# A fused mLSTM, leaky MoE layer and top-1 MoE: the gates' pieces stored before the weight conversions, first loads reordered, and the front's schedule drawn anew

## The chip, the cores and the metric

One core of a Trainium2 chip. Times are device microseconds (us) of one execution. PE is TensorE (matmuls; PEld its weight loads), DVE VectorE, ACT ScalarE, POOL GpSimd, SP the engine that here only issues DMAs. ACT and POOL issue DMAs as well.

## The reference

```python
# mLSTM: B, H, S, D = 4, 8, 768, 40; one step per t
m_new = np.maximum(f_gate[:, :, t] + m, i_gate[:, :, t])
f_stab = np.exp(f_gate[:, :, t] + m - m_new); i_stab = np.exp(i_gate[:, :, t] - m_new)
C = f_stab * C + i_stab * einsum('bhd,bhe->bhde', vt, kt)
n = f_stab * n + i_stab * kt
y[:, :, t] = sigmoid(o_gate) * (C @ qt) / max(|n . qt|, 1)
# layer 1: x is (3072, 320), w_in (320, 2048), w_out (2048, 320)
h = x @ w_in; x = (max(h, 0) + alpha * min(h, 0)) @ w_out
# layer 2: expert = argmax of the cosine logits over 8 experts, gate = its softmax weight
out[mask] = gate * (max(x[mask] @ w1[e], 0) @ w2[e])      # w1[e] (320, 1024), w2[e] (1024, 320)
```

## The kernel before, in words

**Three stages.** The tokens are 24 chunks of 128 (6 for each of the 4 batches). Stage one, the mLSTM, works chunk by chunk. Stage two, the leaky layer, works on groups: chunk 0, chunk 1, then pairs of chunks. For group j and k = 0 to 7 the step `m1(j,k)` is 16 or 32 matmuls of the first product (L747); it is followed on ACT by `m1r` (L754), on DVE by two instructions `m1f` (L760, one for each half), on ACT by `m1h` (L764) and on POOL by `m1l` (L767). `m2(j,t,q)` is a quarter of the second product (12 matmuls, L835). Then come the router, a sort of the tokens by expert, and stage three, the experts (L1212, L1232). All products are of float16 pairs (a high and a low part), so nearly every tile is split in two.

**The gates** are done once, for all chunks, at the start. `g_load` brings f_gate and i_gate, `g_scan` (DVE, L295 to L299) makes running sums and maxima. From these come two things. First, each of two rows is cut into three bfloat16 pieces: `g_top` (ACT, L302), `g_res` (DVE, L305), `g_mid` (ACT, L309), `g_low` (DVE, L312), then `g_store` (SP, L315) writes them to `pc_d` in DRAM, and `g_rows` (L319) and `a_mrow` (L421) read them back in another layout as operands of `a_arg`, the first matmul that a chunk's decay matrix needs (L444, L446). Second, `g_w` (L324 to L326), `g_wexp` (ACT, L329), `g_wt` (PE, L336) and `g_wt2` (DVE, L340, L341) make the weights `wuT` and `winT` of the state; `g_dec` (L344) and `g_dec2` (L347) carry a column through DRAM to `decB`.

**A chunk i**: `load` (keys, values, gates: `kvo_t`, L411), `loadt` (queries and keys transposed: `qk`, L417), `arg` and `exp` (ACT, L453), scores `s` (PE, L462), `p` (DVE, L477: scores times decay), `phi` (ACT) and `plo` (POOL) split that, `vhi` and `vlo` (ACT L424, DVE L428) split the values, `vw` (POOL, L437) and `u` (PE, L472) make the state's update, `c` (DVE, L508) the state, `o` (PE, L516 to L523) the output, `tot` (DVE, L538 to L546), `th`, `y`, `yr`, and `xhi`, `xlo`, `xt` (ACT L560, DVE L564 and L566, an SP transpose L571) hand it to stage two. There are 48 `p` in all, two for each chunk.

**The weights of stage two** come as 64-bit floats in 26 pieces. `pload` (ACT's DMA queue, L690) brings a piece into one of 5 buffers, `pconv` turns two pieces into float32 with six DVE instructions (L637, L639, L641: 128x512 for the five pairs of w_in, 128x320 for the eight of w_out; I call one pair a conversion), `psplit` (ACT) and `plow` (POOL) split them, and two pieces with the tail rows of w_in are moved by `pput` (four SP DMAs, L668 to L671). The first steps of group 0 and 1 need their w_in pieces, their `m2` the w_out pieces. The weights of stage three are split in 56 units (`ul`, `uh`, `uo` on DVE at L1156 to L1160, `us`), scattered over stage two.

**What sets the order.** Every step is announced with `add(key, engine, cost, function, after=..., take=..., give=..., dma=..., at=...)`. `Plan.order` then plays a list schedule when the program is built: each step's rank is the longest path of costs behind it plus `lean(k)`, a number for each kind of step from the tables LEAN, SOON (chunks or groups 0 to 3, and steps without an index below 4) and FIRST (0 and 1), and it emits the steps in the order of its own clock. `at` is the earliest time there. On the chip each engine then runs its instructions strictly in that order; costs and ranks only decide the order. Each DMA also takes the next of eight semaphores in turn, so a DMA can't be issued before the one eight places ahead of it in the program has landed.

## Time and profile before

| | |
|---|---|
| median of 3 runs | 726.04 us (726.01 to 727.79) |
| profiled execution | 729.88 us, span 728.2 us |
| mean granted TensorE clock | 0.977 |
| PE busy | 639.3 us, 88% |
| PEld busy | 526.2 us, 72% |
| DVE busy | 470.0 us, 65% |
| ACT, POOL busy | 335.8 us (46%), 352.3 us (48%) |
| HBM | 143.57 MB read, 30.46 MB written, 239 GB/s over the span |

An engine's busy time is an average over stages: the sections below read it by stretches. Times of the trace count from the span's start.

### The profile page before, as it was taken

The page shows a single profiled execution, that of the slowest core. Times are in us where ns is not written, and L with a number is a line of the kernel's source. Part 1 is how long each engine was busy: PE and PEld are TensorE (multiplying, and loading weights), DVE is VectorE, ACT ScalarE, POOL GpSimd, SP SyncE. Part 2 cuts the span into 40 slices and gives each one's busy share as a digit, 9 for nine tenths or more (in the row PEclk, how much of TensorE's full clock was granted, in tenths as well). Part 3 has the DMA queues.
Part 4 walks back from the last instruction along what each step waited for, and adds up shares of the span by engine and source line. Part 5 has one row for each costly group of instructions (what it writes and reads, how often), then busy time and mean ns, then how long its engine had stood idle before and what let it go on. Part 6 is the DMA issues. An engine that isn't in the chain of part 4 may idle for free. (4 is left out here: it accounts for less than half of the span.)

```text
span 728.2 us, 17807 instructions
## 1 busy us (share of the span) xinstructions
PE 639.3 (88%) x6903; PEld 526.2 (72%) x6903; DVE 470.0 (65%) x1119; ACT 335.8 (46%) x666; POOL 352.3 (48%) x424
## 2 busy tenths in 40 slices
PE   1038468999999989999999999999989999989995
PEld 1025457778887867787878778887777888878884
DVE  8647997798888878888787888797145321112111
ACT  2434466666756576566665655344122222212221
POOL 6647575875646455656465646246112322323322
PEclk9997779999999999999999999999999999999999
DMA  8964343968869687868767675366793999999863
GB/s 233 210 181 136 123 136 82 230 194 197 226 179 292 164 232 184 250 202 247 204 216 220 197 207 163 84 272 153 199 269 86 258 287 282 296 283 340 206 198 69
DMA packets 107306, 149.03 MB, mean 205 GB/s; under 512 B 70295, under 2 KB 82496, under 8 KB 103378
## 3 DMA queue, kind: packets, MB, share of 16 engines
q1 hardware_dynamic: 79810, 83.22, 44.0%
q10 hardware_dynamic: 24128, 54.54, 23.8%
q0 software_dynamic: 3280, 10.10, 5.2%
q8 instruction: 56, 0.92, 0.5%
q14 instruction: 32, 0.26, 0.1%
HBM read 143.57 MB, written 30.46 MB: 239 GB/s over the span
## 5 line engine op out<-in xcount | busy, mean ns | idle before, releaser
L747 PE MATMUL hp<-xt,w_in_p 128*128 128x256 f16 (+1 forms) x1664 | 187.4, 268 | 16.3 <-DVE r L760 7.9
L747 PEld LDWEIGHTS <-w_in_p 128*128 128x128 f16 x1664 | 151.6, 100 | 39.5 <-DVE r L760 14.4
L767 POOL TENSOR_TENSOR g<-r,g 128x512 f16<-128x512 f32 (+1 forms) x104 | 122.6, 1185 | 112.4 <-ACT g L764 109.3
L835 PE MATMUL o<-w_out_p,g 128*128 128x320 f16 x1152 | 169.5, 299 | 0.0
L835 PEld LDWEIGHTS <-g 128*128 128x128 f16 x1152 | 111.8, 98 | 41.9
L1221 DVE SCALAR_TENSOR_TENSOR h<-hp,h 128x512 f16<-128x512 f32 x48 | 32.9, 690 | 114.3 <-ACT h L1217 114.3
L760 DVE SCALAR_TENSOR_TENSOR r<-r,al,hp 128x256 f32<-128x256 f32 (+1 forms) x208 | 84.6, 452 | 26.3 <-ACT r L754 26.0
L764 ACT ACTIVATE g<-r 128x512 f16<-128x512 f32 (+1 forms) x104 | 61.7, 595 | 76.4 <-DVE r L760 63.7
L485 POOL TENSOR_TENSOR ph<-mb,ph 128x512 f16<-128x512 f32 x48 | 63.2, 1323 | 41.3 <-ACT ph L482 40.6
L1232 PEld LDWEIGHTS <-h 128*128 128x128 f16 x648 | 61.8, 98 | 27.1 <-issue 4.4
L754 ACT ACTIVATE r<-hp 128x512 f32<-128x512 f32 (+1 forms) x104 | 57.5, 555 | 26.8 <-PE hp L747 20.7
L1217 ACT ACTIVATE h<-hp 128x512 f16<-128x512 f32 x48 | 28.3, 596 | 86.4 <-PE hp L1212 86.2
L1238 POOL DMA_INDIRECT out_dram<-y,idx x27 | 27.5, 1017 | 82.7 <-DMA out_dram<-y,idx 65.4
L1187 POOL DMA_INDIRECT xg<-x_d,idx x31 | 30.5, 985 | 57.6 <-ACT y L1235 51.9
L1212 PEld LDWEIGHTS <-wr 128*128 128x128 f16 x896 | 51.8, 98 | 2.6 <-issue 1.2
L1212 PEld LDWEIGHTS <-w_in_p 128*128 128x128 f16 x832 | 48.3, 98 | 1.4
L1212 PE MATMUL hp<-xt,wr 128*128 128x128 f16 x768 | 46.8, 219 | 1.0 <-ACT y L1235 0.6
L1212 PE MATMUL hp<-xt,w_in_p 128*128 128x128 f16 x768 | 46.8, 219 | 0.0
L1232 PE MATMUL o<-wr,h 128*128 128x320 f16 x288 | 42.9, 299 | 3.4 <-DMA wr<-wp 2.0
L1232 PE MATMUL o<-w_out_p,h 128*128 128x320 f16 x288 | 43.0, 299 | 1.1 <-DVE h L1221 0.6
L462 PE MATMUL sp<-qk 64*128 64x128 f32 x384 | 29.8, 293 | 15.3 <-DMA qk<-in_qk_t_dram 13.6
L472 PE MATMUL up<-vw,kvo_t 128*128 128x82 f32 x160 | 23.1, 292 | 22.1 <-POOL vw L438 16.0
(206 smaller groups left out, 1027.6 us busy)
## 6 DMA issues: line engine op xcount, KB each, us to landing
wr<-wp SPq DMA_DIRECT2D x32, 1280.0 KB
w_in_p<-wp SPq DMA_DIRECT2D x15, 1280.0 KB
w_out_p<-wp SPq DMA_DIRECT2D x15, 1280.0 KB
kvo_t<-in_kvo_dram SPq DMA_DIRECT2D x24, 576.0 KB
ust<-in_moe_w_dram ACTq DMA_DIRECT2D x32, 320.0 KB
wp<-wo ACTq DMA_DIRECT2D x32, 320.0 KB
ust<-in_moe_w_dram ACTq DMA_DIRECT2D x16, 512.0 KB
wp<-wo ACTq DMA_DIRECT2D x16, 512.0 KB
```

What stands on the lines that cost most here:

```text
L462: T.matmul(sp[:, r, z], lhsT=x[w, 1, z], rhs=x[w, 0, z], start=True, stop=True)
L485: G.tensor_tensor(st["P", i][:, 1, j], st["mb", i][:, j], st["P", i][:, 0, j], ALU.subtract)
L747: T.matmul(hp[:, a, :n], lhsT=w_in_p[:, wk, f], rhs=xt[:, xk], start=z == 0, stop=z == 7)
L754: A.activation(r, e_t[j, m], AF.Relu, scale=-1.0)
L760: V.scalar_tensor_tensor(r[:, a], r[:, a], al1[:, m + a:m + a + 1], hp[:, a], ALU.mult, ALU.add)
L764: A.activation(g_t[j][:, 0, m:m + 2], e_t[j, m], AF.Copy)
L767: G.tensor_tensor(g_t[j][:, 1, m:m + 2], e_t.pop((j, m)), g_t[j][:, 0, m:m + 2], ALU.subtract)
L835: T.matmul(o[:, :DM], lhsT=g[:, gi, k, tt], rhs=w_out_p[:, k, a], start=z == 0, stop=z == 47)
L1187: G.indirect_dma_start(out=xg, out_offset=None, in_=src, in_offset=bass.IndirectOffsetOnAxis(ap=idx[:, j:j + 1].bitcast(U32), axis=0))
L1212: T.matmul(hp[:, m], lhsT=w[:, wk, f], rhs=xt[:, xk], start=z == 0, stop=z == 7)
L1221: V.scalar_tensor_tensor(hs[:, 1], hp, 0.0, hs[:, 0], ALU.max, ALU.subtract)
L1232: T.matmul(o, lhsT=h[:, hi, k], rhs=w[:, k, a], start=z == 0, stop=z == 23)
```

## The change

Seven edits, all but the second and the third in what the plan is told:

- `g_low(1)` comes behind `g_low(0)`, and the first `pconv` behind `g_low(1)` in the list of dependences of piece 0's pair; the tables LEAN, SOON and FIRST have new numbers throughout, and some costs are raised.
- `g_w` runs on DVE and not on POOL.
- `xhi` and `x2_hi` write the 64 columns DM to DM+64 by a second ACT instruction, straight from their source; the DVE copies at L566 and L905 go.
- `load(i)` and `loadt(i)` wait for `load(i-1)` and `loadt(i-1)` in the plan, and those of chunks 1 and 2 are not placed before 14 and 26.
- `g_dec2` waits for `g_rows`.
- `alpha`, `rload` and `x2zero` are held to 20, 75 and 75, `consts` (the sort's constants) to 200.
- The units are told to start at 132.6 with 5.47 between them (115.5 and 5.75 before), with 2.07 (6.16) as the gap of their DVE steps.

```diff
-    START = {"T": 0.5, "V": 7.0, "A": 1.0, "G": 8.0, "S": 1.0}
+    START = {"T": 0.5, "V": 9.3, "A": 1.0, "G": 8.0, "S": 1.0}
...
 LEAN = {
-    "alpha": 150, "alpha2": 111.9, "arg0": -42.1, "arg1": -22.1, "c": 12.3, "cd": -127.5, "consts": -37.5,
+    "alpha": 82.5, "alpha2": 101, "arg0": -42.5, "arg1": -18.3, "c": -57.9, "cd": -81.1, "consts": -111.5,
...
-PACE = 6.16
-UNITS = (115.5, 5.75)
+PACE = 2.07
+UNITS = (132.6, 5.47)
...
-        G.tensor_tensor(mprev, last, gc[:, :NC_ - 1, P - 1:P], ALU.add)
-        G.tensor_tensor(ww[:, 1], aa[:, :NC_ - 1, :], last.to_broadcast([32, NC_ - 1, P]), ALU.subtract)
-        G.tensor_tensor(ww[:, 0], mprev.to_broadcast([32, NC_ - 1, P]), mm[:, 1:, :], ALU.subtract)
+        V.tensor_tensor(mprev, last, gc[:, :NC_ - 1, P - 1:P], ALU.add)
+        V.tensor_tensor(ww[:, 1], aa[:, :NC_ - 1, :], last.to_broadcast([32, NC_ - 1, P]), ALU.subtract)
+        V.tensor_tensor(ww[:, 0], mprev.to_broadcast([32, NC_ - 1, P]), mm[:, 1:, :], ALU.subtract)
...
-        A.activation(xs[i % NB][:, 0:DM], st["y", i], AF.Copy, scale=128.0)
+        x, y = xs[i % NB], st["y", i]
+        A.activation(x[:, 0:DM], y, AF.Copy, scale=128.0)
+        A.activation(x[:, DM:DM + 64], y[:, DM - 64:], AF.Copy, scale=128.0)
...
-        V.tensor_copy(x[:, DM:DM + 64], x[:, DM - 64:DM])
...
-          + ([("u", i - 3)] if (i - 3) % NC_ < NC_ - 1 else []), dma=1.8)
-        a("loadt", "S", 0.78, a_loadt, [(n, i - NQ) for n in ("s", "o")], dma=1.0)
+          + ([("u", i - 3)] if (i - 3) % NC_ < NC_ - 1 else []) + [("load", i - 1), ("loadt", i - 1)], dma=2.2, at=(0.0, 14.0, 26.0)[i] if i < 3 else 0.0)
+        a("loadt", "S", 0.78, a_loadt, [(n, i - NQ) for n in ("s", "o")] + [("load", i - 1), ("loadt", i - 1)], dma=1.2, at=(0.0, 14.0, 26.0)[i] if i < 3 else 0.0)
...
-                add(("pconv", z // 2), "V", 0.3 + 2.75 * c, p_conv, z, z + 1, after=[("pload", z), ("pload", z + 1)],
+                add(("pconv", z // 2), "V", 0.3 + 2.75 * c, p_conv, z, z + 1, after=[("pload", z), ("pload", z + 1)] + ([] if z else [("g_low", 1)]),
...
-        add(("g_low", a), "V", 0.85, g_low, a, after=[("g_mid", a)])
+        add(("g_low", a), "V", 0.95, g_low, a, after=[("g_mid", a)] + ([("g_low", 0)] if a else []))
...
-    add(("g_w",), "G", 5.3, g_w, after=[("g_scan",)])
+    add(("g_w",), "V", 2.2, g_w, after=[("g_scan",)])
...
-    add(("g_dec2",), "S", 3.0, g_dec2, after=[("g_dec",)], dma=0.3)
-    add(("alpha",), "S", 0.6, alpha_load, dma=0.1)
+    add(("g_dec2",), "S", 0.5, g_dec2, after=[("g_dec",), ("g_rows",)], dma=0.3)
+    add(("alpha",), "S", 0.4, alpha_load, dma=0.1, at=20.0)
...
-    add(("rload",), "S", 0.76, load_router, dma=0.1)
+    add(("rload",), "S", 0.76, load_router, dma=0.1, at=75.0)
...
-    add(("consts",), "G", 3.0, sort_consts, at=100.0)
+    add(("consts",), "G", 3.0, sort_consts, at=200.0)
```

What this does to the order shows on SP first: the program's start, just behind the program's entry, up to the third or fourth chunk load. Before (the two gates, then `qk` of chunks 0, 2 and 1, then `kvo_t`):

```order
L1288 DMA al_153<-in_moe_alpha_dram 128x16
L286 DMA gates_a<-in_f_gate_dram 32x768
L287 DMA gates_a<-in_i_gate_dram 32x768
L417 DMA qk_102<-in_qk_t_dram 40x1024 x2
L417 DMA qk_104<-in_qk_t_dram 40x1024 x2
L417 DMA qk_103<-in_qk_t_dram 40x1024 x2
L411 DMA kvo_t<-in_kvo_dram 128x1152 x2
L868 DMA em<-in_moe_expert_emb_dram 8x320
```

The changed program at the same place, and on to the gates' stores and their reading back:

```order
L286 DMA gates_a<-in_f_gate_dram 32x768
L287 DMA gates_a<-in_i_gate_dram 32x768
L411 DMA kvo_t<-in_kvo_dram 128x1152
L417 DMA qk_102<-in_qk_t_dram 40x1024 x2
L411 DMA kvo_t<-in_kvo_dram 128x1152
L417 DMA qk_103<-in_qk_t_dram 40x1024 x2
L344 DMA dec_d<-gates_b 32x4x1
L1289 DMA al_153<-in_moe_alpha_dram 128x16
L315 DMA pc_d<-gates_a 32x6x768
```

Chunk 0's `kvo_t` has moved from behind nine DMAs to the third place, and `alpha` and the router's loads have left the start. The next place on SP is the store of the pieces (`pc_d`) and its reading back. Before, it stands behind `decB` and the router's transpose, some DMAs later:

```order
L344 DMA dec_d<-gates_b 32x4x1
L892 DMA_TRANSPOSE enp<-ep 128x5x128
L347 DMA decB<-dec_d 128x128
L315 DMA pc_d<-gates_a 32x6x768
L319 DMA argL<-pc_d 8x4x768 x3
L421 DMA argR_113<-pc_d 3x8x128
```

In the changed program, from the store on:

```order
L315 DMA pc_d<-gates_a 32x6x768
L669 DMA w_in_p<-ttl 64x512
L670 DMA w_in_p<-ttl 64x512
L671 DMA w_in_p<-ttl 64x512
L672 DMA w_in_p<-ttl 64x512
L417 DMA qk_104<-in_qk_t_dram 40x1024 x2
L421 DMA argR_113<-pc_d 3x8x128
L319 DMA argL<-pc_d 8x4x768 x3
L421 DMA argR_114<-pc_d 3x8x128
L411 DMA kvo_t<-in_kvo_dram 128x1152
L347 DMA decB<-dec_d 128x128
```

The store now stands ahead of `decB`, which follows the reading back, and the four DMAs of one tail piece and chunk 2's `qk` stand between the store and the reading back. On DVE the place is the end of the gates' work. Before, the last instructions ahead of `wuT` are those of a fourth conversion:

```order
L639 SCALAR_TENSOR_TENSOR w_335<-wst,w_335 128x512
L639 SCALAR_TENSOR_TENSOR w_336<-wst,w_336 128x512
L641 SCALAR_TENSOR_TENSOR w_335<-wst,w_335 128x512
L641 SCALAR_TENSOR_TENSOR w_336<-wst,w_336 128x512
L340 TENSOR_SCALAR wuT<-gps 128x160
L341 COPY winT<-gps 128x160
L477 SCALAR_TENSOR_TENSOR mb<-sp,mb 128x512 x2
```

In the changed program one conversion (w_253 and w_254) stands ahead of `wuT`, between `g_res` and `g_low`:

```order
L642 SCALAR_TENSOR_TENSOR w_253<-wst,w_253 128x512
L642 SCALAR_TENSOR_TENSOR w_254<-wst,w_254 128x512
L312 TENSOR_TENSOR gates_a<-gates_a 32x768
L428 SCALAR_TENSOR_TENSOR vs_106<-kvo_t,vs_106 128x8x40
L312 TENSOR_TENSOR gates_a<-gates_b,gates_a 32x768
L1292 TENSOR_SCALAR al_153<-al_153 128x16
L340 TENSOR_SCALAR wuT<-gps 128x160
L341 COPY winT<-gps 128x160
L638 TENSOR_SCALAR w_287<-wst 128x512
```

Ahead of these rows DVE has, behind `g_scan`: `vlo(0)`, the three instructions of `g_w`, the two of `g_res` and the first conversion. Three more conversions follow before chunk 0's `tot` (L541), the third between chunk 0's two `p`; before the change five conversions of 128x512 and one of 128x320 and the router's eleven instructions (L880 to L888) stood ahead of that `tot`. ACT's first instructions are now `vhi(0)` and `th(0)`, then `g_top` twice, `g_wexp` and `g_mid` twice.

## Rows read from the trace of the kernel before

**Rows 1.** Stretches: length; busy (count) of PE, PEld, DVE, ACT, POOL; clock; DMA share, GB/s.
```profile
0.00:48.06 48.06, 6.10 (x34) 5.19 (x34) 32.50 (x61) 16.21 (x27) 31.26 (x50) 1.00 0.88 211
48.06:60.31 12.25, 8.53 (x48) 3.86 (x48) 9.44 (x14) 7.02 (x15) 5.47 (x5) 0.86 0.42 128
60.31:123.91 63.60, 44.16 (x494) 37.62 (x494) 54.53 (x121) 33.06 (x81) 43.06 (x103) 0.79 0.46 130
...
200.00:500.00 300.00, 292.58 (x2900) 236.90 (x2898) 246.19 (x603) 174.09 (x335) 158.59 (x152) 1.00 0.70 204
```

**Rows 2.** Waits of PE up to 124 us: total, times, longest.
```profile
PE up L472 <- POOL vw L438: 16.0, 1, 16.0
...
PE ap L444 <- DMA argR<-pc_d: 4.3, 1, 4.3
```

**Rows 3.** SP's timeline: start, length, and the DMAs issued.
```profile
13.35 3.76 SPq L411 DMA_DIRECT2D kvo_t<-in_kvo_dram  x2
...
29.62 0.53 SPq L344 DMA_DIRECT2D dec_d<-gates_b  x1
...
37.18 0.34 SPq L347 DMA_DIRECT2D decB<-dec_d  x1
37.61 0.85 SPq L315 DMA_DIRECT2D pc_d<-gates_a  x1
44.54 1.09 SPq L319 DMA_DIRECT2D argL<-pc_d  x3
```

**Rows 4.** DVE's timeline: start, length, instruction.
```profile
11.47 0.15 DVE L298 COPY gates_a<-gates_a 32x5 f32<-32x5 f32 x1
...
13.33 0.72 DVE L637 TENSOR_SCALAR w<-wst 128x512 int32<-128x512 int32 x2
...
16.40 0.94 DVE L305 SCALAR_TENSOR_TENSOR gates_a<-gates_b,gates_a 32x768 f32<-32x768 f32 x1
...
29.69 0.94 DVE L312 TENSOR_TENSOR gates_a<-gates_b,gates_a 32x768 bf16<-32x768 f32 x1
...
40.54 0.31 DVE L340 TENSOR_SCALAR wuT<-gps 128x160 f32<-128x160 f32 x1
...
60.31 0.49 DVE L541 COPY tot<-op 128x328 f32<-128x328 f32 x1
...
123.03 0.88 DVE L641 SCALAR_TENSOR_TENSOR w<-wst,w 128x320 int32<-128x320 int32 x2
```

**Rows 5.** Timelines of POOL, ACT, ACT and PE: one instruction each.
```profile
13.49 4.78 POOL L324 TENSOR_TENSOR gates_b<-gates_b,gates_a 32x5 f32<-32x5 f32 x1 [4.75 <-DVE gates_b L299]
...
23.28 1.25 ACT L329 ACTIVATE gates_b<-gates_b 32x1280 f32<-32x1280 f32 x1
...
27.03 0.47 ACT L528 ACTIVATE th<-kvo_t 128x320 f32<-128x320 f32 x1 [1.86 <-DMA kvo_t<-in_kvo_dram]
...
48.18 0.58 PE L444 MATMUL ap<-argR,argL 128*128 128x512 bf16 x1 [4.33 <-DMA argR<-pc_d]
```

**Rows 6.** DVE's groups from 60.4 to 123.9 us: count, busy, mean ns.
```profile
L639 DVE SCALAR_TENSOR_TENSOR w<-wst,w 128x320 int32<-128x320 int32 x14 | 10.4, 780 | 0.0
L641 DVE SCALAR_TENSOR_TENSOR w<-wst,w 128x320 int32<-128x320 int32 x14 | 7.7, 588 | 0.0
L637 DVE TENSOR_SCALAR w<-wst 128x320 int32<-128x320 int32 x14 | 6.8, 522 | 0.0
L760 DVE SCALAR_TENSOR_TENSOR r<-r,al,hp 128x128 f32<-128x128 f32 x23 | 6.6, 335 | 3.9 <-ACT r L754 3.9
L477 DVE SCALAR_TENSOR_TENSOR mb<-sp,mb 128x512 f32<-128x512 f32 x8 | 5.3, 687 | 0.1
...
L566 DVE COPY xs<-xs 128x64 f16<-128x64 f16 x3 | 2.5, 818 | 0.0
```

**Rows 7.** All of L1160 on DVE, and one step of the first layer on PE.
```profile
L1160 DVE SCALAR_TENSOR_TENSOR wo<-ust,wo x32: 785/826/1784, 161.2 to 456.1; 128x640 f16<-128x640 f32 x32
...
87.69 1.07 PE L747 MATMUL hp<-xt,w_in_p 128*128 128x128 f16 x16
```

More of the change, by code (lines that the diff above doesn't have):

```diff
@@ L153 @@
 LEAN = {
-    "alpha": 150, "alpha2": 111.9, "arg0": -42.1, "arg1": -22.1, "c": 12.3, "cd": -127.5, "consts": -37.5,
-    "e1": -117.8, "e2": -27.1, "ehi": 117.1, "elo": -12.1, "eout": -93.7, "ep": 93, "exp0": 51.5, "exp1":
-    -85.8, "ey": 64.4, "g_dec": -70.5, "g_dec2": 140.3, "g_load": -8.4, "g_low": -25.6, "g_mid": -22.1,
-    "g_res": 136, "g_rows": 3.5, "g_scan": -136, "g_store": -150, "g_top": -126.8, "g_w": -33.5, "g_wexp":
-    -148.7, "g_wt": 127, "g_wt2": -143.3, "gate": 52.5, "lane": 112.3, "lanes": -71.9, "load": -23.1, "loadt":
[3 rows of a table removed]
@@ L172 @@
-    "g_scan": -28.5, "g_store": 49.2, "g_top": -51.9, "g_w": 74.8, "g_wexp": 50, "g_wt": 6.5, "g_wt2": 68.8,
-    "gate": -20.4, "lane": 77.8, "lanes": -28.8, "load": -80, "loadt": -4.4, "logits": 14.2, "m1": 80, "m1f":
-    -80, "m1h": 62, "m1l": -61.5, "m1r": -20.8, "m2": 5.6, "max": 76.8, "mrow": -80, "norm": -24.3, "norm2":
-    -62.3, "o": 23.2, "open": -3.2, "p0": 35, "p1": 61.3, "pconv": 22.9, "phi0": 28.8, "phi1": -14, "plo0":
-    64.2, "plo1": 80, "pload": 53.6, "plow": 8.3, "pput": -80, "psplit": -53.3, "rank": -20.2, "rexp": 30.8,
@@ L182 @@
 }
 FIRST = {
-    "alpha": -26.9, "alpha2": -28.1, "arg0": 50.2, "arg1": 37.2, "c": -80, "cd": -60.3, "consts": 80, "e1":
-    -56.3, "e2": 69, "ehi": -52.9, "elo": 80, "eout": 36.9, "ep": 25.3, "exp0": -48.3, "exp1": 63.7, "ey":
-    68.1, "g_dec": -56.9, "g_dec2": -45.2, "g_load": -42, "g_low": -49, "g_mid": 49.2, "g_res": 43.1,
-    "g_rows": -11, "g_scan": -0.9, "g_store": 53.3, "g_top": 80, "g_w": 55.3, "g_wexp": -57, "g_wt": -62.6,
-    "g_wt2": -5.6, "gate": -72.4, "lane": 80, "lanes": 58.1, "load": -70.2, "loadt": -9.3, "logits": -80,
@@ new lines @@
+    -28.9, "e2": -55.3, "ehi": 75.1, "elo": 50.8, "eout": 24.6, "ep": -9.1, "exp0": -43.4, "exp1": -79.1,
+    "ey": 18.5, "g_dec": -51.6, "g_dec2": 15.4, "g_load": 72.7, "g_low": -3.5, "g_mid": 21.1, "g_res": 63.2,
+    "g_rows": 64.3, "g_scan": -31.3, "g_store": 4.1, "g_top": 51.8, "g_w": -53.3, "g_wexp": 80, "g_wt": -7.4,
+    "g_wt2": 72.4, "gate": -80, "lane": -51.3, "lanes": 53.3, "load": 31.4, "loadt": -38.2, "logits": -80,
+    "m1": 24.1, "m1f": 22.5, "m1h": -74.5, "m1l": 12.2, "m1r": 60.2, "m2": 23.7, "max": 41.9, "mrow": -44.1,
@@ L576, in plan_chunk, with a @@
         back = i - 1 if i and (i - 1) % NC_ < NC_ - 1 else i - 2
-        def a(name, eng, cost, fn, after, *args, dma=0.0, take=(), give=()):
-            add((name, i), eng, cost, fn, i, *args, dma=dma, take=take, give=give,
+        def a(name, eng, cost, fn, after, *args, dma=0.0, take=(), give=(), at=0.0):
+            add((name, i), eng, cost, fn, i, *args, dma=dma, take=take, give=give, at=at,
                 after=[d if isinstance(d[0], str) and len(d) != 2 else d for d in after
```

45 lines of the change are left out of this document (27 added, 18 removed), and 30 rows, old and new, of tables (FIRST, LEAN, SOON).

## The prediction

> **What bounds the kernel now.** I read the stretches first [rows 1]. From 200 to 500 us PE is busy 292.6 of 300 us: there PE's own work sets the time, and no other engine is near its limit (DVE 246.2, ACT 174.1). Before 123.91 us it is otherwise. PE works 6.1 of the first 48.06 us, 8.5 of the next 12.25 and 44.2 of the next 63.60, so 65 us of the run's idle PE time lie ahead of 123.91. In the third of these stretches DVE is busy 54.5 of 63.6 us: there DVE is the bound, its work being the weight conversions, the chunks and the `m1f`. In the first it is busy 32.5 of 48.06, and nothing is: something late holds everybody.
>
> What is late is found in three views. PE's longest wait is 16.0 us for `vw` [rows 2], which waits for `wuT`; DVE makes that at 40.54 [rows 4], although its input left ACT at 23.28 + 1.25 = 24.5 [rows 5]. DVE runs in order, and conversions stood ahead of it. The second is the decay: PE's first `arg` starts at 48.18 and had waited 4.3 us for DRAM rows [rows 2, 5]. The pieces' last `g_low` ended at 29.69 + 0.94 = 30.6 [rows 4], yet SP issued their store at 37.61, because `decB` stood ahead of it on SP and was not issued before 37.18, when `dec_d`, issued at 29.62, had landed; the reading back was issued at 44.54, when the store had landed [rows 3]. The third is the sum of chunk 0, `tot`, at 60.31, 12.1 us behind `arg`; from it to the end of the last conversion at 123.03 + 0.88 = 123.9 are 63.6 us [rows 4].
>
> **The change, step by step.** *To the store.* The scan ends at 13.3, since the conversion at 13.33 starts right behind it [rows 4]. Then DVE has `vlo(0)`, 0.5, as another instruction of that width takes 0.49 [rows 4]; the 32x5 instruction of `g_w`; and two of 32x640, which I take at 0.8 each, from 0.94 for 32x768 [rows 4]. The trace has no DVE row for that 32x5 subtraction: on POOL it took 4.78 us [rows 5], a DVE copy of the same shape 0.15 [rows 4]. I take 0.15, the row on the engine it moves to. `g_w` then ends at 15.6, `g_wexp` at 16.9 instead of 24.5. With two `g_res` of 0.94, one conversion of 3.07 (13.33 to 16.40) and `g_low`, `vlo(1)`, `g_low` (2.4) DVE reaches 23.0, and SP issues the store there and not at 37.61. `wuT` comes at about 23.2 and not at 40.54.
>
> The Trainium skill bears on this choice: SBUF — State Buffer, section "Who interferes with whom", says that DVE and GpSimd share a pair of ports as an exclusive lock, and that the loser is blocked for a whole instruction. By it the 4.78 us were POOL locked out by the conversion (POOL began at 13.49, DVE's conversion at 13.33), and the sum keeps 0.15. Were 4.78 the instruction's own length, the store would come 4.6 us later and the sum below be 4.6 us less. No run here has shown that instruction alone.
>
> *To the first `arg`.* From the store's issue to PE's `arg` it was 48.18 - 37.61 = 10.6 us [rows 3, 5]. Now four DMAs of a tail piece, two of `qk` and one `argR` stand between, and one part of the reading back needs a weight load issued at about 27 (behind the second conversion) to have landed, by the eight semaphores. I add 1 us: 23.0 + 10.6 + 1.0 = 34.6, a lead of 13.6. Bounds: 33.6 with nothing added; 44.3 if that load takes 13.7 us, as the first `kvo_t` did (13.35 to its first use at 27.03 [rows 3, 5]), with 3.6 us from the reading back to `arg`. I stay near the low end: six weight loads and six `qk` were issued ahead of that `kvo_t`, but at 27 only three weight loads and the store are young.
>
> *To `tot` of chunk 0.* 12.1 us before; DVE filled at least 9.44 - 1.4 = 8.0 of them with two conversions between the two `p` and `tot` [rows 1, 6]. Now one of 3.07 stands there, so 7.1 us at best; POOL's split and PE's products then show, and I take 9.0: `tot` at 43.6, not 60.31.
>
> *From there to the last conversion.* By the order of the instructions up to the last conversion, DVE has the same thirteen conversions, `vlo`, `c`, `tot`, `y` and `xlo` as before, 12 `p` for 10, 32 `m1f` for 22, and no copies. What lay ahead of `tot` and now lies behind it: one conversion of 128x320 (1.9 by width from the 3.07; 2 x (0.78 + 0.59 + 0.52) = 3.8 in this stretch [rows 6]), one of 128x512 (3.1 bare, 6.1 by that ratio) and the router's eleven instructions, some 2.5 us, an estimate at 0.23 each, between the small rows of 0.15 and 0.31 [rows 4]. New: two `p` at 0.69 and ten `m1f` at 0.34, 4.7 us. Gone: three copies, 2.5 us [rows 6]. Together +9.7 to +14.6; I take 12, between them, since POOL, whose work these instructions meet in the rows, stays as busy. Then 54.5 + 12 = 66.5 us of work, and of the 9.1 us in which DVE was not busy I keep 6 (bounds 0 and 9.1): the order is new, but the engines that it waits for are the same. The last conversion ends at 43.6 + 66.5 + 6 = 116.1, 7.8 earlier (bounds 105, with `arg` at 33.6, and 125).
>
> *What PE has then.* Ten `m1f` more are five `m1` steps of 1.07 us [rows 7], 5.4 us, and the scores of one more chunk, some 1.1 (one step's time, estimate): PE is 6.5 us further at that point. Behind it PE's own work sets the time, so both count: 7.8 + 6.5 = 14.3 us.
>
> *Edits at nothing.* The second ACT instruction of `xhi` and `x2_hi`, 48 of at most 0.47 (ACT's 128x320 [rows 5]), lies in ACT's 42% of idle time from 200 to 500; uncovered it would delay each `xlo` by 0.47, which PE sees only where it waits for DVE. The 48 copies that go free DVE where it doesn't set the time; a gain there is possible, and I count none. `decB` now waits behind the reading back; its first reader, `cd(1)`, comes after `c(0)`, which waits for `u(0)` only, so an issue at 33 would delay chunk 1's state, not chunk 0's `tot`. The early `kvo_t` (third DMA, issued at about 1.8) stands ahead of the gate chain on ACT (`vhi`, `th`) and DVE (`vlo`): if it lands by 12 nothing waits; if it takes 13.7 us again it lands at 15.5 and the chain slips by 3. I take no slip, as only 0.2 MB of its own queue is ahead of it. The constants held back free SP and POOL at the start, and the router's transpose finds its time before the first `x2_hi`.
>
> The sum is 729.88 - 14.3 = 715.6 for the profiled execution. That execution is 3.84 above the median of the three runs, so the forecast for the median is 726.04 - 14.3 = **711.7 us**. A measurement of this kernel can tell about 0.3%, 2.2 us, from no change.
>
> **The rivals.** *The loads eat the lead.* The weight load of the reading back takes 13.7 us, `arg` starts at 44.3 and 9.7 of the lead go: gain 4.6, 721.4 us. For it: the share of 0.88 in the first stretch [rows 1]; against: chunk 2's loads and the constants' have moved out of the start.
>
> *DVE's stretch also gets denser.* With `wuT` 17 us earlier and PE's first `m1` as early, DVE's waits in the third stretch go (9.1 us [rows 1]), and the additions cost only 9.7: 6 + 2.3 more, gain 22.6, 703.4 us. For it: 3.9 of those are `m1f` waiting for ACT [rows 6], and ten `m1f` more by then say that PE runs further ahead; against: the chunks' own chain is not shortened.
>
> *The units fall behind: slower.* The units' commonest instruction (L1160, four of each seven) runs from 161.2 to 456.1, 52 intervals of 5.67 us for 53 units [rows 7]. In DVE's new order the first unit comes behind 42 `m1f` and not 30 (the twelve between are the stretch from 139 to 152 before), and the last behind 176 as before, so the units must run at about (295 - 13) / 52 = 5.42 us. The experts' weights and the sort wait for the last one. If the queues could give only one in 5.9 us, the last would come 25 us late and the run take 729.88 - 14.3 + 25 = 740.6, 736.7 by the median; it decides from 5.42 + 16.5/52 = 5.74 us on. Against: the DMA share is 0.70 and ACT's 58% in that stretch [rows 1], and DVE loses the copies.
>
> *The plan's order moves nothing on the chip.* PE's first real work would have to wait for something not seen, at 48 as before: 726. I see no such thing.
>
> **How the numbers follow.** Likeliest, 0.60: 711.7, its own range 706 to 719 (DVE's idle 0 to 9.1, the additions 9.7 to 14.6, `arg` 33.6 to 38). Denser, 0.15: 703. Loads, 0.13: 721. Nothing, 0.05: 726. Units, 0.07: 737. Faster by over 0.3% is 0.60 + 0.15 + 0.13 = 0.88, the same 0.05, slower 0.07. A range from 703 to 722 holds the first three but for the ends, some 8 in 10.
>
> **What would show it.** In the changed trace: the 32x5 subtraction on DVE under 0.3 us; the store's issue near 23, `arg` near 35, `tot` of chunk 0 near 44, the last conversion near 116 with 32 `m1f` ahead of it, and PE's idle time up to there some 15 us less. From 200 to 500 PE should be as busy as now. Wrong would be: `vhi(0)` waiting for `kvo_t` beyond 14, `argL` issued near 41, or new PE waits for experts' weights (`wr`) near 510.

## The result, and the profile after

| | before | after |
|---|---|---|
| median | 726.91 us (726.01 to 730.14) | 735.88 us (733.83 to 739.52) |
| profiled execution, span | 729.88, 728.2 | 735.27, 733.6 |
| PE, DVE, ACT, POOL busy | 639.3, 470.0, 335.8, 352.3 | 644.6, 464.4, 343.6, 339.9 |

The ratio is 1.0138 [1.0100, 1.0176] (in brackets the 95% interval, here and below): 1.4% slower, where 711.7 us (703 to 722) was predicted. Single executions of one kernel on one chip differ by 1 to 3%, and the chips of the experiments differ (the kernel before had medians of 725.05, 726.14, 726.02 and 729.99 us on four of them), so kernels are compared by their ratio to the kernel before on the same chip; disturbed executions are left out of it, so that it isn't always the ratio of the two medians. Lines of the changed kernel stand one higher than before (L760 is L761).

The stretches of [rows 1] in the changed kernel, and behind them the stretch from the first `tot` to the last conversion's end (columns as there):

```profile
0.00:48.06 48.06, 14.93 (x94) 10.44 (x96) 37.35 (x57) 20.98 (x36) 24.78 (x50) 1.00 0.77 226
48.06:60.31 12.25, 6.44 (x30) 4.31 (x27) 9.68 (x22) 7.02 (x15) 7.16 (x8) 0.65 0.44 146
60.31:123.91 63.60, 46.60 (x550) 40.33 (x550) 55.77 (x130) 36.87 (x95) 41.30 (x50) 0.83 0.44 116
123.91:200.00 76.09, 72.36 (x740) 59.22 (x738) 65.66 (x141) 48.62 (x103) 50.69 (x53) 1.00 0.74 209
200.00:500.00 300.00, 287.10 (x2791) 231.44 (x2790) 233.69 (x559) 174.13 (x359) 151.24 (x198) 0.99 0.72 201
...
46.74:122.41 75.67, 52.30 (x557) 44.19 (x557) 65.84 (x152) 43.13 (x107) 49.35 (x57) 0.80 0.46 127
```

The front did win: PE works 14.9 us of the first 48 (6.1 before). The loss stands in the fifth line: from 200 to 500 PE is busy 287.1 us, 5.5 less than before, and it was to be "as busy as now".

The steps of [rows 3 to 5] as the timelines of SP, of PE and of DVE have them now, then two of PE's waits in the first 62 us ([rows 2]; its longest there is 13.1 us for the first `qk`, 12.7 before), and two of DVE's groups from 46.7 to 122.5 us ([rows 6]):

```profile
22.26 0.32 SPq L315 DMA_DIRECT2D pc_d<-gates_a  x1
...
30.24 2.83 SPq L319 DMA_DIRECT2D argL<-pc_d  x3
```

```profile
36.52 0.58 PE L444 MATMUL ap<-argR,argL 128*128 128x512 bf16 x1 [8.74 <-DMA argL<-pc_d]
```

```profile
13.62 0.15 DVE L324 TENSOR_TENSOR gates_b<-gates_b,gates_a 32x5 f32<-32x5 f32 x1
...
24.27 0.31 DVE L340 TENSOR_SCALAR wuT<-gps 128x160 f32<-128x160 f32 x1
...
46.74 0.50 DVE L541 COPY tot<-op 128x328 f32<-128x328 f32 x1 [2.64 <-PE op L523]
...
121.53 0.88 DVE L642 SCALAR_TENSOR_TENSOR w<-wst,w 128x320 int32<-128x320 int32 x2
```

```profile
PE ap L444 <- DMA argL<-pc_d: 8.7, 1, 8.7
PE up L472 <- POOL vw L438: 7.6, 1, 7.6
```

```profile
L761 DVE SCALAR_TENSOR_TENSOR r<-r,al,hp 128x128 f32<-128x128 f32 x32 | 9.1, 337 | 2.1 <-ACT r L755 2.1
...
L566 DVE SCALAR_TENSOR_TENSOR xs<-y,xs 128x320 f16<-128x320 f32 x4 | 3.0, 747 | 2.5 <-ACT xs L561 2.5
```

So the store is issued 15.4 us earlier, `arg` starts 11.7 and `tot` 13.6 earlier, and PE's wait for `vw` is 7.6 for 16.0; but the last conversion ends only 1.5 earlier (122.4 for 123.9). The 32 `m1f` forecast ahead of it are there (L761, x32). The profile before is a late one at this point: in six profiles with its front `arg` starts at 43.3 to 48.2 and `tot` at 55.4 to 60.3, and it has the latest of both. Over all profiles the new front leads at `tot` by 7 to 13.6 us.

One view more is needed, since PE's busy time is not its progress. I gave each matmul of the program the median step between two neighbours of its form (603.4 us in all, the same in each kernel), and added them up to a moment. The difference to the kernel before at the same moment is PE's **lead** in us; one profiled execution each:

```
us               48   124   140   200   240   260   300   500   640   700
changed        +5.4  +7.5  +8.9  +4.8  +2.1  -1.6  -0.6  -3.0  -2.0  -5.3
```

PE is 7.5 us ahead at 124 and 8.9 at 140, loses 10.5 from there to 260, and 3.3 from 640 to 700. The span is longer by 5.4. Two more profiles (after_again and new_tail_old below) are of the same program up to 522 us. Up to 240 they differ from this one by at most 0.7 us; behind that they have +1.9 and +4.5 at 260 and +0.7 and +3.0 at 500, so that a lead read there from one profile is uncertain by some 6 us.

### The profile page after: what moved, and what is told of

Read it like the earlier page. It is cut to its first block, busy times and chain, and to the rows that moved or that the text cites. A ratio compares the mean times of both kernels' runs of the same rounds, so it can differ in the third digit from the quotient of the medians.

```text
span 733.6 us, 17830 instructions
## 1 busy us (share of the span) xinstructions
PE 644.6 (88%) x6903; PEld 530.2 (72%) x6903; DVE 464.4 (63%) x1074; ACT 343.6 (47%) x714; POOL 339.9 (46%) x421
## 3 DMA queue, kind: packets, MB, share of 16 engines
q1 hardware_dynamic: 79810, 83.22, 44.3%
## 5 line engine op out<-in xcount | busy, mean ns | idle before, releaser
L768 POOL TENSOR_TENSOR g<-r,g 128x512 f16<-128x512 f32 (+1 forms) x104 | 120.0, 1163 | 107.3 <-ACT g L765 105.1
L761 DVE SCALAR_TENSOR_TENSOR r<-r,al,hp 128x256 f32<-128x256 f32 (+1 forms) x208 | 83.8, 452 | 23.2 <-ACT r L755 22.8
L1213 PEld LDWEIGHTS <-w_in_p 128*128 128x128 f16 x832 | 48.2, 98 | 1.7 <-issue 0.4
L462 PE MATMUL sp<-qk 64*128 64x128 f32 x384 | 31.4, 304 | 16.3 <-DMA qk<-in_qk_t_dram 14.1
L462 PEld LDWEIGHTS sp<-qk 64*128 64x128 f32 x384 | 26.3, 204 | 22.3 <-issue 18.1
L453 ACT ACTIVATE mb<-ap 128x512 f32<-128x512 f32 x48 | 28.0, 591 | 20.9 <-POOL ph L485 7.2
```

Source lines behind the costliest of these rows:

```text
L462: T.matmul(sp[:, r, z], lhsT=x[w, 1, z], rhs=x[w, 0, z], start=True, stop=True)
L761: V.scalar_tensor_tensor(r[:, a], r[:, a], al1[:, m + a:m + a + 1], hp[:, a], ALU.mult, ALU.add)
L768: G.tensor_tensor(g_t[j][:, 1, m:m + 2], e_t.pop((j, m)), g_t[j][:, 0, m:m + 2], ALU.subtract)
L1213: T.matmul(hp[:, m], lhsT=w[:, wk, f], rhs=xt[:, xk], start=z == 0, stop=z == 7)
```

## Where the lead went, read from the two traces

Stretches of the kernel before and then of the changed kernel (columns as above):

```profile
140.00:200.00 60.00, 59.59 (x608) 49.46 (x605) 53.15 (x129) 40.99 (x82) 39.42 (x38) 1.00 0.80 209
...
225.00:260.00 35.00, 32.84 (x341) 26.49 (x337) 30.47 (x69) 21.58 (x43) 19.94 (x19) 1.00 0.72 216
```

```profile
140.00:200.00 60.00, 56.27 (x580) 46.42 (x579) 54.29 (x116) 40.12 (x82) 37.99 (x37) 1.00 0.76 220
200.00:225.00 25.00, 24.05 (x240) 19.57 (x239) 21.89 (x47) 14.94 (x34) 14.33 (x68) 1.00 0.63 187
225.00:260.00 35.00, 30.84 (x271) 23.18 (x269) 20.84 (x43) 18.66 (x41) 14.00 (x14) 0.90 0.81 188
```

From 140 to 260 PE idles 3.7, 1.0 and 4.2 us, 8.8 in all, before 0.4 + 0 + 2.2 = 2.6: 6.3 more. The granted clock falls to 0.90 of full speed in the last 35 us, at most 3.5 us of work. Together up to 9.8 of the 10.5. What ended PE's waits in these 120 us of the changed kernel (total, times, longest):

```profile
PE op L516 <- ACT cf L506: 3.1, 1, 3.1
PE hp L748 <- DVE r L761: 1.8, 1, 1.8
PE sp L462 <- issue: 1.3, 1, 1.3
PE op L523 <- POOL ph L485: 0.7, 1, 0.7
```

The 3.1 has a chain behind it, in ACT's timeline and then PE's:

```profile
230.33 0.48 ACTq L1134 DMA_DIRECT2D ust<-in_moe_w_dram  x1
236.84 0.47 ACTq L1135 DMA_DIRECT2D ust<-in_moe_w_dram  x1
237.36 0.60 ACT L453 ACTIVATE mb<-ap 128x512 f32<-128x512 f32 x1 [6.43 <-DMA xt<-xs]
...
242.97 0.61 ACT L506 ACTIVATE cf<-up 64x164 f32<-64x164 f32 x2
```

```profile
243.64 2.00 PE L516 MATMUL op<-cf,qk 128*128 128x82 f32 x8 [3.08 <-ACT cf L506]
```

ACT issues a unit's two loads. The second must take the next of eight semaphores, which a transpose `xt`, issued by SP at 227.37, still held. ACT stood 6.4 us, DVE 5.7 us behind it, and the state's `cf` came 3 us late for PE. This stall differs from execution to execution: in new_tail_old, the same program up to here, ACT stood 3.0 us, PE waited 0.5 us for `cf`, and it idled 0.3 us from 240 to 260, where it idles 3.1 here. From 140 to 240 the two idle alike, 5.8 us.

In the tail PE waits for the experts' weights, 2.0 us before and 5.8 now:

```profile
PE o L1233 <- DMA wr<-wp: 5.8, 2, 3.3
```

## The experiments

All but two are the changed kernel's code with its steps emitted from a list written out in the program. NEW is the order of the changed kernel's plan, OLD that of the kernel before; `upto(A, B, s)` is A up to and with step s (`ahead`: without it) and then B's order for the steps that are left, `move(L, steps, s)` puts steps behind s. Two theories stand against each other from the start: **the front was worth nothing** (whatever leads early is lost, since something else sets the pace), and **the middle lost it** (the new order of the units and chunks behind the front costs more than the front gives).

**One half of the order each, and the old order with the new code.**

```diff
-    for k in plan.order():
+    for k in upto(NEW, OLD, ("tot", 0)):      # front_new_rest_old
+    for k in upto(OLD, NEW, ("tot", 0)):      # front_old_rest_new
+    for k in OLD:                             # old_order_new_code
```

> The changed kernel's code; its order of steps up to chunk 0's tot (L541, 46.7 us in the changed trace), then all other steps in the order of the kernel before. Theory (the front's lead was real and the new order behind it spent it: PE's work, counted in matmuls, is 5.4 us ahead at 48 us, 8.9 ahead at 140 and 3.0 behind at 500): tot stays near 47, the last conversion ends near 47 + 64 = 111 to 116, PE keeps 7 to 12 us of lead to the end, 715 to 720 us. Rival (something behind the front, the units or PE, ends at its own time whatever the front does): 724 to 729.

> The changed kernel's code; the order of the kernel before up to chunk 0's tot, then the changed order. Theory (the rest of the new order is what costs): tot near 60 and the new rest's stalls behind it, slower than the changed kernel, 738 to 745 us. Rival (the new rest only takes the time that the front gave): 730 to 736.

> The order of the kernel before in all places, with the changed kernel's code: g_w on DVE where POOL's stood, the 64-column copies on ACT and not on DVE. Theory (the direct edits cost nothing where they stand): 724 to 728 us, PE as busy from 200 to 500 as before (292 us). Rival (the 48 instructions more on ACT, 0.22 us each in the changed trace, lengthen each chunk's way from yr to xt, and that is where PE's time went): 730 to 736.

Measured: front_new_rest_old 730.33 us, 1.0062 [1.0023, 1.0101]; front_old_rest_new 733.84, 1.0109 [1.0053, 1.0165]; old_order_new_code 722.50, 0.9961 [0.9928, 0.9993]. So the edits outside the order (`g_w` on DVE, ACT's copies) cost nothing and may give 0.4%, the new order from the first `tot` on costs 1.1% with the old front, and my 715 to 720 for the new front fell. So did my 738 to 745 for the old front: 733.84 is the rival's. The trace of front_new_rest_old shows a seam that is no part of the change: OLD has the router's constants next, and they stand between `tot` and `y` of chunk 0 on DVE:

```profile
47.10 0.50 DVE L541 COPY tot<-op 128x328 f32<-128x328 f32 x1 [3.02 <-PE op L523]
...
49.71 0.33 DVE L881 MEMSET ep<- 128x320 uint32 x1 [1.46 <-ACT sqe L874]
...
50.63 1.62 DVE L885 TENSOR_SCALAR em<-em,nr 8x320 f32<-8x320 f32 x1
...
58.69 0.47 DVE L552 SCALAR_TENSOR_TENSOR y<-th,tot 128x320 f32<-128x320 f32 x1
```

In the changed kernel that `y` starts at 53.35. A second profile of front_new_rest_old, beside a second one of the changed kernel:

> The kernel with the changed front and the old rest once more: its profiled execution was the fastest of its twelve (722.6 against a median of 730.3). Theory (DMA packets take longer in some executions, and a transpose or a load that PE or ACT waits for then lands late): a slower execution shows one or more waits of 3 to 6 us for an x2t, xt or expert load between 165 and 300 us, with half clock behind it, and the same lead of 2.5 us at 140. Rival (the front itself differs from execution to execution): the lead at 140 is missing.

> The changed kernel once more, instruction for instruction. Between the changed kernel and the one with the old tail the first 522 us are the same program, yet one lost 3.7 us of PE's lead between 240 and 260 us and the other none, so a part of what one profile shows is that execution's own. Theory: what repeats is the lead of 8 to 10 us at 140 and the waits for wr of 5 us or more behind 620; the wait of ACT's queue at 231 to 238 repeats in most but not all executions. Rival: the waits for wr are missing here too.

Times 727.77 and 736.46, one each, and 736.26 for the kernel before on that chip, also one. The changed kernel's trace repeats: lead 7.4 at 124, 4.8 at 200, ACT's wait 5.63 at 234.82, `wr` 3.9 in the tail; only 250 to 500 went better (+0.7 at 500). The other's second profile has none of the waits of 3 to 6 us that I had expected (1.5 at most from 140 to 300) and a lead of only 1.4 at 140, so neither theory came out clean.

**The seam taken away.** The router's steps behind the ninth of the thirteen conversions (the text on record says the last one; they came at 84.5):

```diff
-    for k in upto(NEW, OLD, ("tot", 0)):
+    for k in move(upto(NEW, OLD, ("tot", 0)), ROUTER, ("pconv", 8)):   # front_new_router_late
```

> The kernel with the changed front up to tot and the old rest, where the router's constants fell right behind tot (47.6 to 53.5 us on DVE), now with those six steps behind the last conversion. Theory (DVE's sum of work sets the pace to some 200 us, in whatever order): y of chunk 0 comes 5 us earlier, near 53.5, the last conversion some 5 earlier, but the router's 3 to 6 us come back behind it: PE's lead at 200 grows by under 2 us and the time is that of the kernel with the router's constants ahead, 727 to 732. Rival (the constants on the way to y(0) are what spoiled the new front there): 720 to 725.

722.38, 0.9954 [0.9918, 0.9989], against 1.0062 with the seam. The router's constants on the way to the first `y` cost 1.1%, the rival's answer. But the new front with the old middle is then no better than the old order throughout (0.9961): `tot` at 48.4 in its profile and at 59.8 in old_order_new_code, 11 us apart, make no difference that can be measured.

**The store's order alone**, in the old order, without and with the router late:

```diff
-    for k in OLD:
+    S = move(OLD, [("g_store",), ("g_rows",)], ("g_low", 1))     # last g_low
+    S = move(move(S, [("g_dec2",)], ("mrow", 1)), [("g_wt2",)], ("vlo", 1))
+    for k in S:                                   # old_store_first
+    for k in move(S, ROUTER, ("pconv", 8)):       # store_first_router_late
```

> The changed code in the old order, with four steps moved: the store of the gates' pieces and the reading back stand right behind the last g_low on SP, decB behind both argR, and wuT (g_wt2) ahead of the two conversions that kept it to 40.5. DVE has done the same conversions when it comes to chunk 0. Theory (only idle time of DVE counts ahead of the last conversion, and DVE waits 9.3 us for the first exponential in this order): arg comes some 6 us earlier, that wait falls to about 3, the last conversion ends near 118, 715 to 719 us. Rival (what DVE gains there it loses again before 124): 721 to 724.

> The old order with the store ahead (0.9945 of the kernel before), and the router's constants moved behind the last conversion, out of the stretch ahead of the last g_low. Theory (DVE was not idle there, so the store and chunk 0 come some 2.5 us earlier and the work comes back behind 116): 721 to 725, not to be told from the kernel without this move. Rival (each us by which the store is earlier counts): 718 to 721.

722.91, 0.9945 [0.9911, 0.9980], and 722.09, 0.9917 [0.9883, 0.9951]. The second, SP's and PE's timelines:

```profile
27.05 0.34 SPq L315 DMA_DIRECT2D pc_d<-gates_a  x1
34.68 1.05 SPq L319 DMA_DIRECT2D argL<-pc_d  x3
```

```profile
41.08 0.58 PE L444 MATMUL ap<-argR,argL 128*128 128x512 bf16 x1 [2.87 <-DMA argL<-pc_d]
```

`arg` starts 7.1 us earlier than in the profile before, 2.2 earlier than in the earliest of the six with the old store; both beat the kernel before by 0.6 to 0.8%, and over the same code in the old order (0.9961) their gain is not resolved.

**ACT's copies alone**, in the kernel before:

```diff
-        A.activation(xs[i % NB][:, 0:DM], st["y", i], AF.Copy, scale=128.0)
+        x, y = xs[i % NB], st["y", i]
+        A.activation(x[:, 0:DM], y, AF.Copy, scale=128.0)
+        A.activation(x[:, DM:DM + 64], y[:, DM - 64:], AF.Copy, scale=128.0)
...
-        V.tensor_copy(x[:, DM:DM + 64], x[:, DM - 64:DM])
... (and the same in x2_hi)
```

> The kernel before with one edit: the 48 copies of 64 columns as ACT instructions, g_w still on POOL, order as before. With the old order and both direct edits the ratio was 0.996. Theory (the copies lie in idle time on either engine, the small gain is g_w's): 724 to 727 us. Rival (taking 48 instructions off DVE is worth something, since DVE is near its limit to 200 us): 720 to 723.

724.08, 0.9977 [0.9943, 1.0011]: no difference, as the prediction priced it.

**Is DVE's work what sets the pace up to the last conversion?** The first of the three conversion instructions is done twice (26 more, 8.0 us):

```diff
-        for t, u, v in dst:
+        for t, u, v in dst + dst:
             V.tensor_scalar(u, t[:, :, 1], 3, 0x3FFFFFF8, ALU.logical_shift_left, ALU.bitwise_and)
```

> The changed kernel with DVE work added and nothing else: the first instruction of each of the thirteen conversions (L638) is issued twice, 26 instructions, 5 x 0.72 + 8 x 0.55 = 8.0 us by the changed trace's own rows, all ahead of the last conversion. Theory (from chunk 0 to the last conversion, and on to some 200 us, DVE's own work sets the pace, so that chunk 0 coming earlier gives nothing): the last conversion ends 6 to 10 us later than 122.4 and the whole is 5 to 9 us slower than the changed kernel, 740 to 744. Rival (DVE has cover there, as its idle time of 12 us from 48 to 122 would allow, and something else gave the lead away): under 3 us slower, 734 to 738.

742.50 (731.63 to 750.71, six), 1.0125 [1.0051, 1.0199]; against 1.0138 of the changed kernel the time can't tell. The trace can:

```profile
127.74 0.89 DVE L642 SCALAR_TENSOR_TENSOR w<-wst,w 128x320 int32<-128x320 int32 x2
```

The last conversion ends at 128.6, 6.2 later for 8.0 more, and PE's lead at 124 is 3.1 for 7.5: up to there, DVE's work reaches PE. At 500 the lead is -6.7, for -3.0 and +0.7 in the two profiles of the changed kernel, so that the loss lasts is a hint and not shown.

**Where the middle begins and ends.**

```diff
-    for k in plan.order():
+    for k in ahead(NEW, OLD, ("ul", 0, 0)):   # new_to_units: NEW ahead of the first unit's load
+    for k in upto(OLD, NEW, ("m1", 5, 7)):    # old_to_280: OLD up to 280 us
```

> The changed code; the changed order up to the last step ahead of the first expert unit's load, then the order of the kernel before. Theory (the changed order bunches chunks 10 to 13 with the units of experts 1 and 2 between 150 and 250 us, and that costs the 8.9 us that PE leads at 140): the lead is kept, PE has 8 us more work done at 300 us than in the kernel before, 714 to 718 us. Rival (the lead at 140 is borrowed: ten m1f and PE's steps were done ahead of DVE work that still has to come, so DVE catches up with any order): PE's lead falls under 3 us by 260, 721 to 727.

> The changed code; the old order up to the last m1 of group 5 (near 280 us), then the changed order to the end. With the old front and the changed tail the changed middle (from tot to the first e1) is 1.0109 of the kernel before and the old middle 0.9905. Theory (the middle loses its time between 60 and 280 us, where the two orders differ most): 719 to 724 us. Rival (it loses behind 280, or the changed tail costs by itself): 727 or more.

new_to_units 732.40, 1.0086 [1.0046, 1.0125], for 714 to 718 expected, but at its seam ACT waited 9 us for unit loads at 137 to 152 and PE's lead fell from 9.6 to -0.9 by 200: it says little. old_to_280 740.74, 1.0143 [1.0108, 1.0178], for 719 to 724 expected; the seam cost 5.4 us at 283 to 290, then 2.8 more went by 500 and 4.5 in waits for `wr`. So part of the loss lies behind 280, but the seams make both poor rulers.

**Two suspects in the middle.** The two loads of the stall moved behind `c(12)`, and the steps that NEW interleaves put in turn, `m1` of groups 5 and 6, `m2` and the router of 3 and 4:

```diff
-    for k in plan.order():
+    for k in move(NEW, [("ul", 2, 2), ("ul", 2, 3)], ("c", 12)):   # unit_load_later
+    for k in in_turn(NEW):        # groups_in_turn: 105 steps change places
```

> The changed kernel with one thing moved: the loads of expert 2's third and fourth unit stand behind the state of chunk 12 (c, L506) on ACT's queue, not ahead of chunk 13's first exponential (L453). Theory (the wait at 230.8 to 236.8 us, where ACT's queue stood at the second half of that load until an earlier transpose on SP had landed, cost PE 3.9 us of idle time and some 2 more at 0.53 of the clock): ACT's 6.4 us of idle time there go, PE's clock stays 1.00 from 240 to 250, 729 to 733 us. Rival (PE's lead or lag is set elsewhere, and the time comes back as other waits): 734 to 737.

> The changed kernel with groups 3 to 6 in turn: the changed order has m2 of group 4 ahead of the last four parts of group 3's, and m1 of group 6 ahead of group 5's, whose buffer of g those parts hold; here the same places of the order are filled group by group, 105 of 2199 steps, chunks and units untouched. Theory (group 5's input is there from about 200 us, so that PE stands at chunk 12's state at 240 us for want of m1 steps that it could have had, and the out-of-turn order is a large part of the middle's loss): PE's idle time and low clock from 225 to 250 us shrink by 3 us or more, 728 to 732 us. Rival (the loss from 140 to 240 is many small waits for DVE): 733 to 737.

unit_load_later 734.21, 1.0112 [1.0057, 1.0168]. ACT no longer stands at the issue but at the data (ACT's waits, 225 to 250 us):

```profile
ACT wo L1148 <- DMA ust<-in_moe_w_dram: 6.3, 1, 6.3
```

The wait moved by one place and kept its length. The two loads were issued at 237.90 and 238.43 here, just ahead of their use, so the run doesn't tell whether their transfers were late or the new place was. groups_in_turn 737.20, 1.0082 [1.0046, 1.0118], an interval that overlaps the changed kernel's, and PE was busy 25.65 us from 225 to 255 for 25.84: not shown.

**The tail.**

```diff
-    for k in plan.order():
+    for k in ahead(NEW, OLD, ("e1", 0, 0)):             # new_tail_old: the experts in OLD's order
+    for k in ahead(OLD, NEW, ("e1", 0, 0)):             # old_order_new_tail
+    for k in ahead(in_turn(NEW), OLD, ("e1", 0, 0)):   # in_turn_tail_old
+    for k in ahead(move(S, ROUTER, ("pconv", 8)), NEW, ("e1", 0, 0)):   # best_of_both
```

> The changed kernel with the steps from the first e1 on (522 us) in the order of the kernel before; the 1847 steps ahead are the same set in both. Theory (the changed tail issues the experts' conditional weight loads later among SP's other transfers, which is why PE waits 5.0 to 6.5 us for wr in all three profiles with that tail and 0 to 2.0 in the three with the old one): the waits for wr fall under 2.5 us, 729 to 732 us. Rival (the waits come from late units or from DMA in general): 734 to 737.

> The old order up to the first e1, the changed order behind it, the changed code: the mirror of the kernel with the new order and the old tail. Theory (the tail's order costs 0.7 to 0.8% by itself): PE waits 3 to 6 us for wr near 670 to 680 us, 726 to 729 us, 4 to 6 above the old order with the new code. Rival (those waits came from the state that the changed order leaves behind at 522 us): 721 to 724, no wait for wr over 2.5 us.

> The same with the steps from the first e1 on in the old order too: the changed order with two of its stretches mended. Theory (both faults add up, and the tail's is there only behind the changed middle): 721 to 726 us. Rival (the old tail alone does it): 728 to 731, like the kernel with the old tail alone.

> The old order with the store and wuT ahead, the router's constants behind the ninth conversion (where the changed order has them), the changed tail from the first e1 on, the changed code. The two kernels of which it is made were 0.9917 and 0.9905 of the kernel before. Theory (their gains are partly of one cause, the code's): 718 to 722 us. Rival (the tail's gain there was chance): 722 to 725.

new_tail_old 729.36, 1.0063 [1.0042, 1.0084]: without the new tail behind the new middle the waits for `wr` are gone, and the ratio is 0.75% below the changed kernel's. old_order_new_tail 721.02, 0.9905 [0.9867, 0.9942]: the same new tail behind the old middle has no wait for `wr` over 0.3 us and costs nothing, so my theory that the tail's order by itself makes them fell. in_turn_tail_old 733.38, 1.0038 [1.0008, 1.0067], not told from new_tail_old. best_of_both 728.39, 0.9980 [0.9959, 1.0001]: I expected 718 to 722 on adding the two best; the gains didn't add, or not on that chip, where its two parts were not run. All four profiles from that chip (old_to_280, groups_in_turn and these last two), and after_again from another, lost 3.8 to 5.0 us at 560 to 600, where PE waited for an issue (`ip`, L1114, 1.3 to 3.6 us); why is not known. The fastest seen are old_order_new_tail and store_first_router_late.

PE in the stretches of old_order_new_tail:

```profile
124.00:200.00 76.00, 75.61 (x771) 61.73 (x769) 61.44 (x145) 51.62 (x110) 51.77 (x54) 1.00 0.81 211
200.00:500.00 300.00, 295.72 (x2923) 240.54 (x2921) 243.71 (x586) 179.22 (x370) 162.50 (x156) 0.99 0.73 205
```

With the changed middle PE worked 72.4 and 287.1 us in these two, with the old one 75.6 and 295.7. Leads of the runs named, as in the first table:

```
us                       48   124   140   200   260   500   640   700
after_again            +5.3  +7.4  +8.9  +4.8  +1.9  +0.7  -3.4  -6.1
front_old_rest_new     +1.7  +6.3  +7.8  +3.6  -1.7  -4.3  -3.9  -9.4
new_tail_old           +5.4  +8.1  +9.6  +5.5  +4.5  +3.0  +3.0  +5.8
front_new_router_late  +4.8  +2.5  +3.9  +4.2  +5.0  +7.2  +7.0  +9.4
old_order_new_tail     +1.7  +2.4  +3.7  +3.5  +5.6  +7.2  +7.7  +9.4
old_order_new_code     +0.2  +0.0  -0.7  -1.1  +0.8  +1.9  +1.9  +3.1
```

Behind 140 us the three runs with the changed middle lose 6.6 to 12.1 by 500, and the three with the old one gain 2.6 to 3.5, whichever front they had. front_old_rest_new also shows that the lead at 124 is the changed order's of the stretch behind `tot`, not the early store's: it has 6.3 with the old front (`tot` at 56.7), and front_new_router_late only 2.5 with the new one.

## Why the prediction was wrong

**The front: right, with two terms too small.** The 32x5 instruction took 0.15 us on DVE, as the sum had it, where POOL had taken 4.78 [rows 5]. The 4.78 was waiting, not work: in act_copies the same instruction stands on POOL at the same moment and takes 0.29 us. POOL's row in act_copies, then DVE's second `g_res` in the kernel before:

```profile
13.49 0.29 POOL L324 TENSOR_TENSOR gates_b<-gates_b,gates_a 32x5 f32<-32x5 f32 x1 [4.75 <-DVE gates_b L299]
```

```profile
17.26 0.94 DVE L305 SCALAR_TENSOR_TENSOR gates_b<-gates_b,gates_a 32x768 f32<-32x768 f32 x1
```

That agrees with the Trainium skill, SBUF — State Buffer, "Who interferes with whom", by which DVE and GpSimd exclude each other from a shared pair of ports. But the conversion alone did not block POOL, as the prediction reads it: the 4.78 us end at 18.27, just behind the second `g_res` (18.20), so it seems to have waited for all eight DVE instructions up to there. The store came at 22.26 (23.0 forecast) and `wuT` at 24.27 (23.2). `arg` came at 36.52 for 34.6, inside the bounds given (33.6 to 44.3), since the reading back was issued 8.0 us behind the store (6.9 before) and its three DMAs took 2.8 us to issue (1.1 before). `tot` came at 46.74 for 43.6, 10.2 us behind `arg` where 9.0 was forecast.

**The stretch to the last conversion: work right, idle wrong.** DVE's work from `tot` to there was 65.84 us, 66.5 forecast. Its idle time was 75.67 - 65.84 = 9.8, and I had kept 6 within bounds of 0 and 9.1. So the end came at 122.4 for 116.1: 3.1 of the 6.3 from `tot`, 3.8 from the idle time, 0.7 back from the work. The ten more `m1f` by then were there, and PE's lead at 124 was 7.5, where 14.3 was forecast. More than a size was off: in the 19 profiles without added work `tot` lies anywhere from 46.7 to 60.3, and the last conversion always ends between 119.0 and 124.7, so an earlier front hardly moves it.

**The step that failed:** "Behind it PE's own work sets the time, so both count." It held for the kernel before, where PE is busy 97.5% of the 300 us [rows 1], and I carried it over to an order in which 2199 steps stand anew. Of the two, the 7.8 us were 1.5; the 6.5 came, with the changed middle behind either front (the leads of front_old_rest_new), and did not last: of a lead of 7.8 to 9.6 at 140, 1.4 to 2.3 are left at 240 in the changed kernel, after_again, new_tail_old and front_old_rest_new. PE idles 5.0 to 6.6 us from 140 to 240 in all eight profiles with that middle. In the kernel before and in seven others with the old middle there it idles 0.0 to 0.5, in three more 2.8 to 4.2, where it waits for one late transpose; new_to_units has its seam in that stretch. Whether the lead was lost to the new order's own waits, or had only been borrowed by doing some of PE's steps ahead of others, the runs don't tell apart.

The comparisons show the price with less of the seams' trouble: front_old_rest_new and old_order_new_tail have the same front and tail and differ only from the first `tot` to the first expert: 1.0109 against 0.9905 (on two chips, each against the kernel before there). The middle costs about 2% there, some 15 us, with the waits for `wr` behind it (6.9 us in the first one's profile); with the new front and the old tail it costs 1.0063 - 0.9954 = 1.1%, and the router's steps stand at nearly the same place in these two (L885 on DVE at 84.2 and 85.1 us). What a step that has moved meets there, another late transfer or another engine's work, I had priced for the units only.

**The rivals.** *The units fall behind* gave 736.7, near the 735.88, but not by its mechanism: the units' commonest instruction runs

```profile
L1161 DVE SCALAR_TENSOR_TENSOR wo<-ust,wo x32: 793/826/1795, 166.3 to 460.5; 128x640 f16<-128x640 f32 x32
```

that is 294.2 us for 52 intervals, 5.66 each as before [rows 7] and not 5.42. The last comes 4.4 us later than before, but the longer waits for `wr` ended at 650.6 and 680.6, not near 510, and PE waited 1.2 us for the sort (`lanes`; 1.0 before). An agreement of the total is no support here. *DVE's stretch gets denser* was wrong: its waits did not go, 9.8 us for 9.1. *The loads eat the lead*: `arg` was 1.9 us later than forecast, not 9.7. *Nothing moves* was wrong for the front.

**Edits at nothing** held: ACT's copies 0.9977 with no difference told, all edits outside the order together 0.9961.

**What stays open.** Which of the middle's waits does it: taking away the largest one's cause at one place moved it (unit_load_later), putting the groups in turn was not resolved. Summed over 140 to 220 us, DVE's instructions took 14.3 to 17.0 us longer than the quickest quarter of their form in all eight profiles with the changed middle, 12.1 in the kernel before and 7.7 to 9.6 in the eleven others, so contention with POOL may be part; that is a hint, and no run varied it alone. And why the new tail waits for `wr` only behind the changed middle (3.9 to 6.9 us in the seven profiles with both, 2.0 at most in the others) is not known: the load that PE waited 3.6 us for in after_again was issued 7.5 us ahead.

## What to carry to other kernels

An earlier start pays only if the engine that bounds the rest stays as busy afterwards, and a full engine in the old order doesn't show that it will be full in a new one: price every stretch that the change puts in a new order, not only the one it aims at. Follow progress in work done, stretch by stretch: it shows where a lead is lost, which neither the total nor a share of busy time tells. A lead is not yet a gain: here it came with the order that then lost it. When an order of thousands of steps is drawn anew, try its front, middle and tail apart, and look at each seam before believing the time; here the front was worth nothing that could be measured, the middle cost 1 to 2%, and the new tail cost only behind that middle.
